# K pairs in four transfers of every fourth partition, with score matmuls that read K in whole lines

## The chip, the cores and the metric

The kernel runs on one core of one Trainium2 chip. The metric is the device time of one launch in microseconds, so lower is better. "Before" took 186.11 us (median of 3 runs, 185.71 to 186.42). For a program on one core, "slow" means over 1.5% above the fastest run of the same kernel.

## The reference

It computes two rounds of attention plus gated MLP, for 4 batches with one query token each. Cut to what matters:

```python
# B=4, D=512, Hq=32, Hkv=8, Sk=8192, Dh=128; window W = 2048 keys; all bf16
def _A_ref(x, k_cache, v_cache, wq, wo):
    q = (x @ wq).reshape(B, 1, 32, 128)
    k = k_cache[:, :, Sk - W:, :]          # repeated for 4 query heads each
    v = v_cache[:, :, Sk - W:, :]
    p = softmax(q k^T * Dh ** -0.5)
    return (p v) @ wo
x = x + _A_ref(layernorm(x), K, V, wq, wo)
x = x + glu(layernorm(x), w_gate, w_up, w_down)   # D=512, F=1792
# ... and both lines once more, with the same K, V and weights
```

K in the window is 4 x 8 x 2048 x 128 x 2 bytes = 16.8 MB, and V is the same. The kernel keeps all of K in SBUF between the two rounds, and reads nearly all of V twice.

## The kernel before

All transfers except the small input x are issued by one engine (SyncE) in a planned order. For each KV head, K comes in two *pairs* of batches, 1 MB per transfer. A pair fills 128 partitions with one 8 KB row (32 keys) each, and neighbouring partitions alternate between the two batches:

```python
def pair_d(cache, h, bp):       # DRAM side: 64 x 2 rows of 8 KB
    return cache[2 * bp:2 * bp + 2, h, SK - W:SK, :].rearrange("b (p j) d -> p b (j d)", p=64)

def load_k(h):
    where[("K", h)] = h
    for bp in range(2):
        dma("K%d_%d" % (h, bp), kpair(h, bp), pair_d(A_k, h, bp), w=tok(4 * h + 2 * bp), rate="bw_8k")
```

VectorE then transposes each tile of 128 x 1024 4-byte words in place (STREAM_TRANSPOSE on the page, 1219 ns each). The score matmuls index what it leaves as blocks in which 32 rows lie side by side along a partition. They read one batch out of the pair:

```python
for cp in range(4):
    for b in range(NB):
        gi = 2 * (b % 2) + b // 2       # four column groups of the array, one per batch
        kt = kpair(hk, b // 2).rearrange("p (j c x i t) -> p c t i j x", c=2, x=16, i=2, t=2)
        q0 = ((k2 * NB + b) * 4 + cp) * NR
        last = pe.matmul(ps[32 * gi:32 * gi + NR, bank, :], qbd[:, q0:q0 + NR],
                         kt[:, cp // 2, cp % 2, b % 2, :, :], start=(cp == 0), stop=(cp == 3))
```

Here `i` is the batch within the pair, and the innermost index `x` steps over it. Successive elements read are 8 bytes apart, so two of them fall into each 16 bytes of a partition. The texts call 16 adjacent bytes of a partition a line; here the word stands for the layout only.

Of the kernel before, what the change touches and what calls it, by code (L numbers as in the profile page):

```python
# [248 lines left out]
class _SlotPool:  # L249
# [12 lines left out]

_TM = dict(
    sem_lat=100.0, pick_tol=60.0,
    dma_issue=60.0, dma_lat0=900.0, dma_lat1=1100.0, dma_max_out=16,
    bw_8k=430.0, bw_4k=412.0, bw_3k=409.0, bw_1k=356.0,
    pe_pair=38.0, pe_small=230.0, pe_f32=450.0, pe_row=80.0, pe_sq=300.0,
    dve_fix=150.0, dve_f32=1.04, dve_small=90.0,
# [4 lines left out]
def build(nc, A_x, A_k, A_v, A_wq, A_wo, B_wg, B_wu, B_wd, out, cfg=None):  # L273
    cfg = dict(cfg or {})
# [4 lines left out]
    KEEP_V = cfg.get("KEEP_V", 2)  # L279
    NG = len(GROUPS)  # L280
    assert GROUPS == [[0, 1, 2, 3]]
    N_DMA_SEMS = cfg.get("N_DMA_SEMS", 24)

    NB, SQ, D = A_x.shape
    _, HKV, SK, DH = A_k.shape
    HQ = A_wq.shape[1] // DH
    REP = HQ // HKV
    W = min(4096, max(256, SK // 4))
# [26 lines left out]
    with es:  # L315
# [35 lines left out]
        eng_sems = dict((e, es.enter_context(nc.semaphore("s_" + e))) for e in ENGINES if e != "sync")  # L351
        dma_sems = [es.enter_context(nc.semaphore("s_dma%d" % i)) for i in range(N_DMA_SEMS)]

# [10 lines left out]
        def slot_ap(s):  # L364
            return arena[:, s * SLOT:(s + 1) * SLOT]

        def tile_ap(s):
            return arena[:, s * SLOT:(s + 2) * SLOT]

        def tok(s):  # L370
            return [("slot", s), ("slot", s + 1)]

        def c_dve(n, rate=None):
            return tm["dve_fix"] + n * (tm["dve_f32"] if rate is None else rate)

        def c_act(n):
            return tm["act_fix"] + n * tm["act_el"]

        def dma(name, dst, src, w, r=(), rate="bw_4k", nbytes=None, sem=None):
            if nbytes is None:  # L380
                nbytes = dst.partition_size() * dst.free_nbytes()
            o = P.op("sync", name, 0.0, lambda e, dst=dst, src=src: e.dma_start(dst, src),  # L382
                     r=r, w=w, dma_bytes=nbytes, dma_rate=tm[rate])
            if sem is not None:
                o.sem = sem
                o.inc = 16
            return o
# [23 lines left out]
        def need(name):  # L411
            while name not in where:
                take_load()
            return where[name]
# [7 lines left out]
        def pair_d(cache, h, bp):  # L422

            return cache[2 * bp:2 * bp + 2, h, SK - W:SK, :].rearrange("b (p j) d -> p b (j d)", p=64)

        def kpair(h, bp):
            return tile_ap(4 * h + 2 * bp)

        def load_k(h):
            where[("K", h)] = h  # L430
            for bp in range(2):
                dma("K%d_%d" % (h, bp), kpair(h, bp), pair_d(A_k, h, bp), w=tok(4 * h + 2 * bp), rate="bw_8k")

        def load(name, n_use, rate, part):
            left[name] = n_use
# [73 lines left out]
        def load_v(h, bp, k, n_use):  # L509
# [7 lines left out]
             r=[("ones_f",)], w=[("ident_b",)])  # L517
# [5 lines left out]
        for jh in range(2):  # L523
            for bp in range(2):
# [7 lines left out]
                     r=[("ones_f",), ("perm",)], w=[("perm", jh, bp)])  # L532
# [5 lines left out]
             r=perms, w=[("sel_f",)])  # L538
        P.op("gpsimd", "sel_b", 200.0, lambda g: g.tensor_copy(sel_b[:, :], sel_f[:, :]),
             r=[("sel_f",)], w=[("sel_b",)])  # L540
        P.op("vector", "sel_r", 100.0,
             lambda v: v.tensor_reduce(sel_r[:, :], sel_f[:, :].rearrange("p (g r) -> p r g", g=4), AXX, ALU.add),
             r=[("sel_f",)], w=[("sel_r",)])
# [4 lines left out]
             r=[("sel_r",)], w=[("maskr",)])  # L548
# [111 lines left out]
        def q_unit(tag, h, k2):  # L660

            for a in range(4):
                dst = qbd[32 * a:32 * a + 32, k2 * 256:(k2 + 1) * 256].rearrange(
                    "p (x y) -> p x y", y=NR)[:, :, a * REP:(a + 1) * REP]
                src = qrep[32 * a:32 * a + 32, h * 64:(h + 1) * 64].rearrange("p (x r) -> p x r", r=REP)
                rd = [("qrep", h // 4)]
                if a % 2 == 0:
                    P.op("vector", "qe%s_%d" % (tag, a), c_dve(64), lambda v, dst=dst, src=src: v.tensor_copy(dst, src),  # L668
                         r=rd, w=[("q", k2, a)])
                else:  # L670
                    P.op("scalar", "qe%s_%d" % (tag, a), c_act(64), lambda s_, dst=dst, src=src: s_.copy(dst, src),  # L671
                         r=rd, w=[("q", k2, a)])

        def k_transpose(h):
            need(("K", h))
            for t in range(4):
                v32 = slot_ap(4 * h + t).bitcast(F32)
                P.op("vector", "T%d_%d" % (h, t), c_dve(1024), lambda v, v32=v32: v.transpose(v32, v32),  # L678
                     r=[("slot", 4 * h + t)], w=[("slot", 4 * h + t)])

        ucount = [0]

        def softmax_unit(tag, hk):
            u = ucount[0]
            ucount[0] += 1
            k2 = u % 2
            bank = SB[k2]
            q_unit(tag, hk, k2)

            def e_s(pe):  # L690
                last = None
                for cp in range(4):
                    for b in range(NB):
                        gi = 2 * (b % 2) + b // 2
                        kt = kpair(hk, b // 2).rearrange("p (j c x i t) -> p c t i j x", c=2, x=16, i=2, t=2)
                        q0 = ((k2 * NB + b) * 4 + cp) * NR
                        last = pe.matmul(ps[32 * gi:32 * gi + NR, bank, :], qbd[:, q0:q0 + NR],  # L697
                                         kt[:, cp // 2, cp % 2, b % 2, :, :], start=(cp == 0), stop=(cp == 3))
                return last
            P.op("tensor", "S" + tag, 16 * tm["pe_row"], e_s,  # L700
                 r=[("slot", 4 * hk + t) for t in range(4)] + [("q", k2, a) for a in range(4)],
                 w=[("pss", k2)], banks=(bank,))
            mk = mxt[:, k2 * 32:(k2 + 1) * 32]
            P.op("vector", "mx" + tag, c_dve(512),
                 lambda v: v.tensor_reduce(nmax[:, k2:k2 + 1], ps[:, bank, :], AXX, ALU.max),  # L705
                 r=[("pss", k2)], w=[("mx", k2)], banks=(bank,))
            P.op("vector", "mk" + tag, tm["dve_small"],
                 lambda v: v.tensor_scalar(mk, maskr[:, :], nmax[:, k2:k2 + 1], None, ALU.add),
                 r=[("mx", k2), ("maskr",)], w=[("mk", k2)])
            P.op("vector", "nm" + tag, tm["dve_small"],  # L710
                 lambda v: v.tensor_reduce(nmax[:, 2 + k2:3 + k2], mk, AXX, ALU.max, negate=True, apply_transpose=True),  # L711
                 r=[("mk", k2)], w=[("nm", k2)])
            P.op("scalar", "ex" + tag, c_act(512) + 200.0,
                 lambda a: a.activation(prow[:, :].rearrange("p (m x t) -> p m x t", x=16, t=2),  # L714
                                        ps[:, bank, :].rearrange("p (m t x) -> p m x t", x=16, t=2), ACTF.Exp, bias=nmax[:, 2 + k2:3 + k2], scale=1.0,
                                        accum_out=psm[:, k2:k2 + 1]),
                 r=[("pss", k2)] + [("nm", k2)], w=[("prow",), ("psm", k2)], banks=(bank,))
            return k2
# [84 lines left out]
        def attn(L):  # L803
            hs = list(range(HKV)) if L == 0 else list(range(HKV))[::-1]

            def front(ui):
                h = hs[ui]
                if L == 0:
                    k_transpose(h)
                k2 = softmax_unit("%d.%d" % (L, ui), h)  # L810
                if L == 2:
                    for bp in range(2):
                        pool.release(4 * h + 2 * bp)
                    fill()
                return k2
# [133 lines left out]
        for h in range(2):  # L949
            loads.append((("K", h), lambda _, h=h: load_k(h)))  # L950
        for h in range(HKV):
            if h + 2 < HKV:
                loads.append((("K", h + 2), lambda _, h=h + 2: load_k(h)))
            if h % 2 == 0:
                load_wo(h // 2)
            for bp in range(2):
                load_v(h, bp, 0, 2 if (h, bp) in keep else 1)
# [25 lines left out]
        order = _schedule(P.ops, tm)  # L983
        counts = _assign_sync(P.ops, order, N_DMA_SEMS)

# [32 lines left out]
def bass_interleave_layers__sliding_block_cached__glu_gated_glu__decode_kernel(  # L1018
    nc, A_x, A_k_cache, A_v_cache, A_wq, A_wo, B_x, B_w_gate, B_w_up, B_w_down, out,
):  # L1020
    build(nc, A_x, A_k_cache, A_v_cache, A_wq, A_wo, B_w_gate, B_w_up, B_w_down, out)
# [28 lines left out]
```

## Time and profile before

| | before |
|---|---|
| time | 186.11 us |
| span of the profiled run | 184.4 us |
| SyncE's transfers (q1), busy share of 16 engines' span | 97.2% |
| bytes moved by q1 | 71.84 MB |
| TensorE busy | 101.2 us (55%) |
| a K or V row of 8 KB on its engine (packet records, median) | 309 to 311 ns |

The page cuts the span into 40 slices: the busy share of the 16 transfer engines in tenths, and what they moved. Below is the slice view with the queue's own line.

```profile
...
DMA  5999999999999999999999999999999999999980
GB/s 198 425 427 427 425 403 391 411 421 419 409 387 425 419 421 403 392 419 419 400 391 414 412 407 393 403 350 417 330 396 419 419 423 416 418 416 402 412 341 24
...
q1 hardware_dynamic: 15352, 71.84, 97.2%
...
```

The queue is full (9) from the second slice on until the last two.

Next, the costliest groups of the page that touch K: score matmuls (L697), the transposes (L678) and the row maximum behind the scores (L705). After the bar come busy us and the mean ns of one, then the idle time before them and who ended it.

```profile
...
L697 PE MATMUL ps<-arena,qbd 128*16 128x512 bf16 x256 | 32.5, 626 | 16.9 <-DVE qbd L668 8.4
...
L678 DVE STREAM_TRANSPOSE arena<-arena 128x1024 f32<-128x1024 f32 x32 | 37.9, 1219 | 3.3 <-DMA arena<-in_A_k_cache_dram 3.0
L705 DVE TENSOR_REDUCE nmax<-ps 128x1 f32<-128x512 f32 x16 | 11.0, 687 | 26.0 <-PE ps L697 26.0
...
```

A busy sum of 32.5 us for score matmuls looks like a target. The chain of waits at the end of the kernel (start, duration, what) shows why it is not one:

```profile
...
164.46 0.89 PE ps L770 x31
165.35 15.77 DMA arena<-in_B_w_down_dram
181.13 0.04 issue
181.17 0.60 PE ps L905 x8
...
```

At 165.35 us a group of matmuls of the second attention ends, and one of the last transfers of weights can be issued. It lands 15.77 us later, behind what is already queued. TensorE meanwhile finishes the attention and does most of the last MLP. With less TensorE time before that point this transfer could be issued earlier, but the transfer engines are full until 178 us (share 1.02 from 165 to 178 us, 0.99 to 1.04 in windows of 2 to 3 us there) and have the same bytes to deliver. So nearly nothing should be won. The page's issue table shows the K transfers (count, KB each, median us from issue to landing):

```profile
...
arena<-in_A_k_cache_dram SPq DMA_DIRECT2D x16, 1024.0 KB, 16.0
...
```

### The profile page before, as it was taken

The page shows a single profiled execution, that of the slowest core. Times are in us where ns is not written, and L with a number is a line of the kernel's source. Part 1 is how long each engine was busy: PE and PEld are TensorE (multiplying, and loading weights), DVE is VectorE, ACT ScalarE, POOL GpSimd, SP SyncE. Part 2 cuts the span into 40 slices and gives each one's busy share as a digit, 9 for nine tenths or more (in the row PEclk, how much of TensorE's full clock was granted, in tenths as well). Part 3 has the DMA queues.
Part 4 walks back from the last instruction along what each step waited for, and adds up shares of the span by engine and source line. Part 5 has one row for each costly group of instructions (what it writes and reads, how often), then busy time and mean ns, then how long its engine had stood idle before and what let it go on. Part 6 is the DMA issues. An engine that isn't in the chain of part 4 may idle for free.

```text
span 184.4 us, 4421 instructions
## 1 busy us (share of the span) xinstructions
PE 101.2 (55%) x1944; PEld 54.7 (30%) x1944; DVE 89.5 (49%) x221; ACT 35.7 (19%) x100; POOL 14.8 (8%) x77
## 2 busy tenths in 40 slices
PE   0532423652807327173373545445979997994474
PEld 0101000332303323023232441210334653584422
DVE  5209998477592565925621531138463442340330
ACT  2003022240212103011020001001365442220010
POOL 4000000110000101010010000000022111120000
PEclk9999995585766756755555555555897897885569
DMA  5999999999999999999999999999999999999980
GB/s 198 425 427 427 425 403 391 411 421 419 409 387 425 419 421 403 392 419 419 400 391 414 412 407 393 403 350 417 330 396 419 419 423 416 418 416 402 412 341 24
DMA packets 15379, 72.12 MB, mean 391 GB/s; under 512 B 1144, under 2 KB 5248, under 8 KB 8704
## 3 DMA queue, kind: packets, MB, share of 16 engines
q1 hardware_dynamic: 15352, 71.84, 97.2%
q8 instruction: 15, 0.25, 0.5%
q14 instruction: 4, 0.03, 0.0%
q10 hardware_dynamic: 8, 0.00, 0.0%
HBM read 71.83 MB, written 0.00 MB: 390 GB/s over the span
## 4 chain that ended last, share of the span: by engine, by line
DMA 52%; PE 25%; SPq 16%; DVE 4%; issue 2%; ACT 0%
DMA arena<-in_A_v_cache_dram 33%; SPq L382 16%; PE ps L697 11%; DMA arena<-in_B_w_down_dram 9%; PE ps L770 8%; DMA arena<-in_A_wq_dram 5%; DMA arena<-in_B_w_up_dram 5%; PE ps L726 2%; PE ps L794 1%; DVE ps L492 1%; PE ps L626 1%; DVE nmax L705 1%; PE ps L749 1%; PE ps L905 1%; PE ps L852 1%
## 5 line engine op out<-in xcount | busy, mean ns | idle before, releaser
L770 PE MATMUL ps<-ebuf,arena 128*128 128x8 bf16 x1024 | 31.0, 167 | 29.7 <-DMA arena<-in_A_v_cache_dram 22.1
L697 PE MATMUL ps<-arena,qbd 128*16 128x512 bf16 x256 | 32.5, 626 | 16.9 <-DVE qbd L668 8.4
L770 PEld LDWEIGHTS ps<-ebuf,arena 128*128 128x128 bf16 x1024 | 28.8, 101 | 36.3 <-DMA arena<-in_A_v_cache_dram 32.5
L678 DVE STREAM_TRANSPOSE arena<-arena 128x1024 f32<-128x1024 f32 x32 | 37.9, 1219 | 3.3 <-DMA arena<-in_A_k_cache_dram 3.0
L705 DVE TENSOR_REDUCE nmax<-ps 128x1 f32<-128x512 f32 x16 | 11.0, 687 | 26.0 <-PE ps L697 26.0
L714 ACT ACTIVATE prow<-ps,nmax 128x512 bf16<-128x512 f32 x16 | 11.0, 687 | 39.6 <-DVE nmax L711 24.9
L671 ACT COPY qbd<-qrep 32x64 bf16<-32x64 bf16 x32 | 7.7, 241 | 40.9 <-PE ps L697 40.3
L697 PEld LDWEIGHTS ps<-arena,qbd 128*16 128x16 bf16 x256 | 6.1, 97 | 31.3 <-issue 22.0
L739 POOL CAST s<-psm 128x1 bf16<-128x1 f32 x16 | 3.0, 188 | 144.4 <-ACT prow L714 144.4
L778 DVE TENSOR_TENSOR onb<-ps,rinv 128x16 bf16<-128x16 f32 x16 | 2.9, 184 | 21.1 <-PE ps L770 21.1
L626 PE MATMUL ps<-arena,xn 128*4 128x512 bf16 x64 | 7.8, 582 | 7.6 <-DMA arena<-in_A_wq_dram 6.2
L794 PE MATMUL ps<-onb,arena 128*128 128x4 bf16 x256 | 9.1, 166 | 3.1 <-DVE onb L778 3.1
L731 ACT CAST prow<-ps 128x512 bf16<-128x512 f32 x16 | 9.4, 587 | 7.1 <-PE ps L726 7.0
L735 DVE STREAM_TRANSPOSE ebuf<-prow 128x256 f32<-128x256 f32 x16 | 7.0, 437 | 6.7 <-ACT prow L731 6.4
L852 PE MATMUL ps<-arena,xn 128*4 128x448 bf16 x64 | 6.5, 560 | 4.9 <-DVE xn L607 3.1
L794 PEld LDWEIGHTS ps<-onb,arena 128*128 128x128 bf16 x256 | 7.9, 101 | 4.1 <-DVE onb L778 2.8
L726 PE MATMUL ps<-prow,perm 64*128 64x256 bf16 x64 | 7.4, 315 | 2.4 <-ACT prow L714 2.3
L596 ACT ACTIVATE lnv<-lnv 128x4 f32<-128x4 f32 x4 | 0.8, 205 | 34.0 <-DVE lnv L593 34.0
L634 DVE STREAM_TRANSPOSE ebuf<-ps 128x512 f32<-128x512 f32 x4 | 2.9, 715 | 7.7 <-PE ps L626 7.6
L859 DVE STREAM_TRANSPOSE ebuf<-ps 128x448 f32<-128x448 f32 x4 | 2.6, 650 | 7.8 <-PE ps L852 7.8
L668 DVE COPY qbd<-qrep 32x64 bf16<-32x64 bf16 x32 | 5.3, 166 | 0.7 <-ACT qrep L657 0.2
L749 PE MATMUL ps<-sel_b,s 128*128 128x16 bf16 x48 | 3.8, 175 | 3.2 <-POOL s L743 2.4
(61 smaller groups left out, 68.1 us busy)
## 6 DMA issues: line engine op xcount, KB each, us to landing
arena<-in_A_v_cache_dram SPq DMA_DIRECT2D x30, 1024.0 KB, 16.8
arena<-in_A_k_cache_dram SPq DMA_DIRECT2D x16, 1024.0 KB, 16.0
arena<-in_A_wq_dram SPq DMA_DIRECT2D x8, 1024.0 KB, 9.4
arena<-in_A_wo_dram SPq DMA_DIRECT2D x4, 1024.0 KB, 24.3
arena<-in_B_w_gate_dram SPq DMA_DIRECT2D x4, 896.0 KB, 19.7
arena<-in_B_w_up_dram SPq DMA_DIRECT2D x4, 896.0 KB, 15.8
arena<-in_B_w_down_dram SPq DMA_DIRECT2D x2, 1024.0 KB, 12.5
arena<-in_B_w_down_dram SPq DMA_DIRECT2D x1, 768.0 KB, 7.0
```

Source lines behind the costliest of these rows:

```text
L382: o = P.op("sync", name, 0.0, lambda e, dst=dst, src=src: e.dma_start(dst, src), r=r, w=w, dma_bytes=nbytes, dma_rate=tm[rate])
L626: last = pe.matmul(ps[32 * hh:32 * hh + NB, qb, :], xn[:, c * NB:(c + 1) * NB], tile_ap(s)[:, o + hh * 512:o + (hh + 1) * 512], start=(c = ...
L671: P.op("scalar", "qe%s_%d" % (tag, a), c_act(64), lambda s_, dst=dst, src=src: s_.copy(dst, src), r=rd, w=[("q", k2, a)])
L678: P.op("vector", "T%d_%d" % (h, t), c_dve(1024), lambda v, v32=v32: v.transpose(v32, v32), r=[("slot", 4 * h + t)], w=[("slot", 4 * h + t)])
L697: last = pe.matmul(ps[32 * gi:32 * gi + NR, bank, :], qbd[:, q0:q0 + NR], kt[:, cp // 2, cp % 2, b % 2, :, :], start=(cp == 0), stop=(cp = ...
L705: lambda v: v.tensor_reduce(nmax[:, k2:k2 + 1], ps[:, bank, :], AXX, ALU.max),
L714: lambda a: a.activation(prow[:, :].rearrange("p (m x t) -> p m x t", x=16, t=2), ps[:, bank, :].rearrange("p (m t x) -> p m x t", x=16, t ...
L726: last = pe.matmul(ps[:, PBS[i], 0:256], perm[64 * i:64 * i + 64, jh * 128:(jh + 1) * 128], prow[64 * i:64 * i + 64, jh * 256:(jh + 1) * 2 ...
L731: lambda a: a.copy(prow[:, :].rearrange("p (y i t) -> p i y t", i=2, t=2), ps[:, PBS[0]:PBS[0] + 2, 0:256].rearrange("p i (y t) -> p i y t ...
L770: last = pe.matmul(ps[:, ob, bp * 8:bp * 8 + 8], src[:, j * 128:(j + 1) * 128], ev[:, j % 2, j % 16 // 2, x0:x0 + 8], start=(j == 0), stop ...
L794: last = pe.matmul(ps[:, WB, c * NB:(c + 1) * NB], tile_ap(s)[:, o + r_ * D + c * 128:o + r_ * D + (c + 1) * 128], ov[:, r_ * NB:(r_ + 1) ...
L852: last = pe.matmul(ps[32 * g:32 * g + NB, OBS[n], 0:NF], xn[:, c * NB:(c + 1) * NB], tile_ap(s)[:, o:o + NF], start=(c == 0), stop=(c == N ...
```

## The change

The intent is to place four partitions of one batch side by side, so that after the transposition four keys of one batch (16 bytes with both halves of a word) are adjacent and score matmuls read K in whole lines. One even step over partitions doesn't give "four of batch 0, four of batch 1" with the batch as an inner dimension of the source. So each pair comes in four transfers, and transfer `x` fills partitions x, x+4, x+8, and so on. The semaphores and the planner's limit rise with the number of transfers.

```diff
-    ... dma_max_out=16,
+    ... dma_max_out=32,
-    N_DMA_SEMS = cfg.get("N_DMA_SEMS", 24)
+    N_DMA_SEMS = cfg.get("N_DMA_SEMS", 40)
@@ load_k
-                dma("K%d_%d" % (h, bp), kpair(h, bp), pair_d(A_k, h, bp), w=tok(4 * h + 2 * bp), rate="bw_8k")
+                src = A_k[2 * bp:2 * bp + 2, h, SK - W:SK, :].rearrange("b (y x j) d -> x y b (j d)", y=16, x=4)
+                for x in range(4):
+                    dma("K%d_%d%d" % (h, bp, x), kpair(h, bp)[x:128:4], src[x], w=[("k", 4 * h + 2 * bp, x)], rate="bw_8k")
@@ k_transpose
-                     r=[("slot", 4 * h + t)], w=[("slot", 4 * h + t)])
+                     r=[("k", 4 * h + t // 2 * 2, x) for x in range(4)], w=[("slot", 4 * h + t)])
@@ softmax_unit
-                        kt = kpair(hk, b // 2).rearrange("p (j c x i t) -> p c t i j x", c=2, x=16, i=2, t=2)
+                        kt = kpair(hk, b // 2).rearrange("p (j c y i x t) -> p c t i j y x", c=2, y=4, i=2, x=4, t=2)
-                                         kt[:, cp // 2, cp % 2, b % 2, :, :], start=(cp == 0), stop=(cp == 3))
+                                         kt[:, cp // 2, cp % 2, b % 2], start=(cp == 0), stop=(cp == 3))
```

More of the change, by code (lines that the diff above doesn't have):

```diff
@@ L264 @@
     sem_lat=100.0, pick_tol=60.0,
-    dma_issue=60.0, dma_lat0=900.0, dma_lat1=1100.0, dma_max_out=16,
+    dma_issue=60.0, dma_lat0=900.0, dma_lat1=1100.0, dma_max_out=32,
     bw_8k=430.0, bw_4k=412.0, bw_3k=409.0, bw_1k=356.0,
```

## The prediction

> **What bounds the kernel.** The DMA does. The page's slices give a DMA share of 9 tenths or more from the second slice to the next to last, and the queue table puts the SyncE queue at 97.2% of 16 engines' span, 71.84 MB. Windows of 4 us show 412 to 428 GB/s almost everywhere while 8 KB rows move, with two dips near 120 us (344) and 128 to 136 us (350). In the packet records an 8 KB row takes 309 ns on its engine and a semaphore write 9 ns. TensorE is busy 55%. The chain of waits names score matmuls (line 697) for 11%, mostly in the second attention (129 to 165 us), but that stretch is followed by a 15.8 us wait for the last weights, which the queue was delivering at full rate all the time: what TensorE saves there only lengthens the queue.
>
> **What the change removes.** Score matmuls now stream a moving operand with four of a line's elements used in a run, not two. A group of 16 lasts 1.9 to 2.0 us now, at granted clock 0.5 (46 us) and 1.0 (129 us) alike, about 480 ns per round of four column groups, so reading, not the clock, sets it.[...] My estimate is 1.0 to 1.7 us after, 0.2 to 0.9 us less in each of 16 groups, 3 to 14 us of TensorE time. Nearly none lies on the binding resource. Earlier slot releases may fill the dip near 120 us: at most 1 us.
>
> **What it adds.** 48 more transfers: 768 semaphore writes at 9 ns over 16 engines, 0.4 us. SyncE pays about 0.61 us per K issue, so 64 take about 39 us, not 10; a 256 KB piece carries 0.62 us of data at 424 GB/s, so the queue keeps its lead of several microseconds, made by wq and V. Vector transposes wait on four semaphores, not one: small.
>
> **The risk** is how 32 rows at a step of four partitions spread over engines.[...] If they collide, K rows take up to twice as long: K is 16.8 MB, 39.6 us at 424 GB/s, so 10 to 30 us more.[...] No transfer in this trace tells.
>
> **Prediction.** Without collisions 185 to 187 us; with them 200 to 215. I put somewhat more on the first: 187.0 us, 8 in 10 between 184.0 and 212.0. Faster by over 2%: 0.05; within 2%: 0.57; slower by over 2%: 0.38.
>
> **What would show it.** Score groups at 1.0 to 1.7 us; DMA share still 9 everywhere; semaphore-write packets up by 768; K issues about 0.6 us each. No collision: 8 KB rows still near 309 ns and 412 to 428 GB/s at 12 to 24 us. Collision: two populations of K rows (309 and up to 620 ns) and 250 to 350 GB/s there, VectorE transposes waiting longer for K.
>
> **What would make it wrong.** SyncE's issue cost rising for a strided destination until the queue runs dry in the first 25 us; a larger cost per small transfer than the 9 ns records show; or the middle of the kernel (104 to 136 us) being so sensitive to early releases that it gains several microseconds.

The sum of the forecast: 185 to 187 us without collisions, 10 to 30 us more with them, put as 200 to 215, and 187.0 us as the middle. The "up to twice as long" is the author's assumption; no transfer of before shows it. The estimate of 1.0 to 1.7 us for a score group is the author's too: no trace of before shows it, and it is not part of the sum (in after, 14 of 16 groups took 1.88 to 1.91 us and two 1.41 and 1.47).

## More of the kernel before

The next view gives two windows of before. The columns are the busy time of each engine with its number of instructions, the granted clock (the share of TensorE's full speed that the profile says it had), the busy share of the transfer engines, and GB/s. In the first window almost only K moves. The second lies around the gated MLP between the two attention rounds.

```profile
...
core 0: us, PE busy (x) PEld busy (x) DVE busy (x) ACT busy (x) POOL busy (x), PEclk, DMA share, GB/s
16.00:24.00 8.00, 2.42 (x32) 0.65 (x32) 7.94 (x10) 1.60 (x7) 0.00 (x0) 1.00 1.01 426
112.00:128.00 16.00, 6.95 (x114) 2.81 (x106) 5.91 (x17) 1.16 (x5) 0.00 (x0) 0.50 1.00 389
...
```

At 426 GB/s and a busy share of 1.01 the transfer engines have no idle time left.

## The result, and the profile after

The change takes **213.84 us** (median of 4 runs, 212.83 to 215.77), against 186.26 us for before in the same rounds. The ratio is 1.1502 (95% interval 1.143 to 1.1574). A ratio here is the mean time of one kernel's fast runs over that of the other's fast runs of the same rounds, so it is not quite the ratio of the medians quoted.

The slice view and queue line of after:

```profile
...
DMA  6999999999999999999999999969999999999990
GB/s 225 420 346 279 279 281 288 411 292 306 350 319 348 350 318 338 258 266 396 283 276 308 348 423 403 377 218 389 360 417 414 412 425 421 418 415 409 406 372 27
...
q1 hardware_dynamic: 16120, 71.84, 96.5%
...
```

The share is still 9 but for the ends and slice 27 (6, near 140 us), but the rate falls to between 258 and 350 GB/s in most slices from the fourth to the 23rd, while K is being loaded. When all K is in SBUF it recovers, and from the 30th slice on it is above 400 until the tail. The engines are as busy as before and move less. Windows of after: the K stretch, and the gated MLP.

```profile
...
core 0: us, PE busy (x) PEld busy (x) DVE busy (x) ACT busy (x) POOL busy (x), PEclk, DMA share, GB/s
16.00:24.00 8.00, 0.64 (x20) 0.41 (x24) 5.07 (x7) 1.27 (x5) 0.00 (x0) 1.00 1.02 281
136.00:152.00 16.00, 7.12 (x110) 3.78 (x108) 4.23 (x20) 1.57 (x7) 0.00 (x0) 1.00 0.83 311
...
```

The K stretch went from 426 to 281 GB/s. The groups that answer to those of before, and the K issues:

```profile
...
L680 DVE STREAM_TRANSPOSE arena<-arena 128x1024 f32<-128x1024 f32 x32 | 38.3, 1225 | 19.1 <-DMA arena<-in_A_k_cache_dram 19.1
...
L699 PE MATMUL ps<-arena,qbd 128*16 128x512 bf16 x256 | 29.3, 602 | 25.7 <-DVE qbd L670 13.0
L707 DVE TENSOR_REDUCE nmax<-ps 128x1 f32<-128x512 f32 x16 | 11.0, 687 | 25.5 <-PE ps L699 25.5
...
```

```profile
...
arena<-in_A_k_cache_dram SPq DMA_DIRECT2D x64, 256.0 KB, 16.8
...
```

VectorE's transposes now wait 19.1 us for K, against 3.0 us before. The score matmuls' busy sum fell only from 32.5 to 29.3 us. The packet records of the trace (one record per row on its engine; counts and durations of the SyncE queue, worked out over the records) show where the time is:

```
                    before: count  median  mean ns  sum/16      after: count  median  mean ns  sum/16
8 KB rows                   6656    311    318.5   132.50 us          6656    316    373.2   155.23 us
1 KB rows                   4100     48     50.3    12.90 us          4100     54     58.2    14.91 us
semaphore writes            1140      9      9.5     0.67 us          1908      9     12.0     1.43 us
8 KB rows, K alone:  before, 12 to 24 us, mean 310.5 ns      after, 16 to 30 us, mean 470.8 ns
```

In this first K stretch of after, all 479 rows lie between 461 and 488 ns. K has 2048 rows, or 128 for each of 16 engines (2048 / 16). If all of them were as slow, 128 x (470.8 - 310.5) ns = 20.5 us would be added; this is an estimate, since later K rows, mixed with V, scatter more. All 8 KB rows together, V included, grew by 22.7 us (155.23 - 132.50). The whole queue was busy for 179.3 us before and for 204.9 us after (the sum of all its records over 16), which is 25.7 us more. The rest of the span difference of 27.9 us is 2.2 us in which the queue was not full; the window 136 to 152 us accounts for it (share 0.83; before had 1.00 in the corresponding window). So nearly all the added time is transfer time, and K rows make about 20 us of it. All 16 engines stay busy in the K stretch (share 1.02), so it isn't that fewer engines do the work.

### The profile page after: what moved, and what is told of

Same layout as the page of the kernel before. It is cut to its first block, busy times and chain, and to the rows that moved or that the text cites. A ratio compares the mean times of both kernels' runs of the same rounds, so it can differ in the third digit from the quotient of the medians.

```text
span 212.3 us, 4510 instructions
## 1 busy us (share of the span) xinstructions
PE 102.0 (48%) x1944; PEld 56.3 (27%) x1944; DVE 90.2 (42%) x221; ACT 35.7 (17%) x100; POOL 14.7 (7%) x77
## 4 chain that ended last, share of the span: by engine, by line
SPq 44%; DMA 33%; PE 17%; issue 3%; DVE 2%; ACT 1%
SPq L382 44%; DMA arena<-in_A_v_cache_dram 16%; DMA arena<-in_B_w_down_dram 12%; PE ps L699 5%; PE ps L772 5%; DMA arena<-in_A_wq_dram 5%; PE ps L728 2%; PE ps L907 1%; PE ps L796 1%; PE ps L628 1%; PE ps L931 0%; PE ps L854 0%; PE ps L751 0%; ACT prow L716 0%; DVE ebuf L636 0%
## 5 line engine op out<-in xcount | busy, mean ns | idle before, releaser
L772 PE MATMUL ps<-ebuf,arena 128*128 128x8 bf16 x1024 | 31.6, 168 | 52.2 <-DMA arena<-in_A_v_cache_dram 49.2
L680 DVE STREAM_TRANSPOSE arena<-arena 128x1024 f32<-128x1024 f32 x32 | 38.3, 1225 | 19.1 <-DMA arena<-in_A_k_cache_dram 19.1
L772 PEld LDWEIGHTS ps<-ebuf,arena 128*128 128x128 bf16 x1024 | 29.4, 104 | 59.1 <-DMA arena<-in_A_v_cache_dram 55.5
L699 PE MATMUL ps<-arena,qbd 128*16 128x512 bf16 x256 | 29.3, 602 | 25.7 <-DVE qbd L670 13.0
L728 PE MATMUL ps<-prow,perm 64*128 64x256 bf16 x64 | 9.3, 389 | 1.4 <-ACT prow L716 1.4
L751 PEld LDWEIGHTS ps<-sel_b,s 128*128 128x128 bf16 x48 | 2.5, 106 | 8.2 <-issue 5.9
```

Of the source, the lines that this page charges most:

```text
L680: P.op("vector", "T%d_%d" % (h, t), c_dve(1024), lambda v, v32=v32: v.transpose(v32, v32), r=[("k", 4 * h + t // 2 * 2, x) for x in range( ...
L728: last = pe.matmul(ps[:, PBS[i], 0:256], perm[64 * i:64 * i + 64, jh * 128:(jh + 1) * 128], prow[64 * i:64 * i + 64, jh * 256:(jh + 1) * 2 ...
L772: last = pe.matmul(ps[:, ob, bp * 8:bp * 8 + 8], src[:, j * 128:(j + 1) * 128], ev[:, j % 2, j % 16 // 2, x0:x0 + 8], start=(j == 0), stop ...
```

## The experiments

Three theories could explain slow K rows:

- **Where rows land.** The record calls it the port theory, and the labels own_port4 and own_port4_again come from it. As a theory: what a row takes depends on the partitions that a transfer fills and on how the rows of its source are given to the engines, which could then get in each other's way. The factors of two and four on 309 ns are assumptions, which the runs test.
- **Small transfers.** 256 KB pieces of 32 rows, or the step of four, cost time in themselves.
- **Memory side.** Neighbouring source rows of a transfer are now 32 KB apart, and reading them so could take longer.

Twelve runs were made, of eleven kernels. Some compute a wrong result. The comparison with the reference passed for all of them, even where keys and values no longer match, so its tolerance does not see such errors here. That own_port4, step2 and quarters are right rests on their layouts, not on this comparison. Several kernels with slow rows scatter by more than 1.5% from run to run, so most of their runs count as "slow". Their runs are then given one by one, and the argument rests on row times and on GB/s inside the K stretch, which differ by far more. Profile lines below are the window 16 to 24 us of each run, with the columns as above. All mean row times are from the packet records in the first stretch of K; another window within it moves the slow means by up to 3 ns.

### own_port4: the same four transfers, source of one dimension

```diff
-  src = A_k[2 * bp:2 * bp + 2, h, SK - W:SK, :].rearrange("b (y x j) d -> x y b (j d)", y=16, x=4)
+  src = A_k[2 * bp:2 * bp + 2, h, SK - W:SK, :].rearrange("b (i x j) d -> b x i (j d)", i=32, x=2)
   for x in range(4):
-      dma(..., kpair(h, bp)[x:128:4], src[x], ...)
+      dma(..., kpair(h, bp)[x:128:4], src[x // 2, x % 2], ...)
@@ score matmuls (two keys of a batch side by side)
+  kt = ... "p (j c y i x t) -> p c t i j y x", c=2, y=8, i=2, x=2, t=2
```

> Still 64 K transfers of 256 KB to every fourth partition, but each takes its 32 rows from one batch, so that the source has one dimension of 32 rows, not 16 x 2. Port theory[...] K rows back to about 309 ns, K stretches at 415 to 430 GB/s, time 185 to 189 us. Small-transfer theory (256 KB pieces or the step of four themselves cost it): K rows stay near 470 ns, 210 to 215 us. Memory-side theory (rows of 16 engines 32 KB apart are slow to read): 16 KB apart here, so some relief, rows 309 to 470 ns.

```profile
...
16.00:24.00 8.00, 2.38 (x32) 0.61 (x32) 7.94 (x10) 1.49 (x6) 0.00 (x0) 1.00 1.02 423
...
```

K rows took 310 ns on average, and the stretch ran at 423 GB/s. The time was 184.71 us (183.94 to 185.5) against 185.91 for before, ratio 0.9944 (0.9896 to 0.9991). There are as many transfers, of the same size, to the same partitions, with as many semaphore writes and issues as in the change, and nothing of the loss is left. The small-transfer theory falls.

### quarters: four transfers to neighbouring partitions

```diff
-  .rearrange("b (y x j) d -> x y b (j d)", y=16, x=4)
+  .rearrange("b (x y j) d -> x y b (j d)", y=16, x=4)
-  kpair(h, bp)[x:128:4]
+  kpair(h, bp)[32 * x:32 * x + 32]          # score reads as before
```

> Four transfers per pair again, but each fills 32 neighbouring partitions with the same pair layout as before, so the result is right and score reads are as before. Port theory:[...] K rows about 618 ns (twice 309), 222 to 230 us. Small-transfer theory: the same as the change, rows 470 ns, 210 to 215 us. Memory-side theory:[...] rows 309 ns, 185 to 189 us.

```profile
...
16.00:24.00 8.00, 0.79 (x32) 0.49 (x32) 3.66 (x5) 1.71 (x6) 0.00 (x0) 1.00 1.02 218
...
```

Rows took 602 ns on average, at 218 GB/s. The time was 234.04 us (232.79 to 237.92, of which the last counts as slow), ratio 1.2576 (1.2512 to 1.264). A transfer fills 32 neighbouring partitions here, and the rows take nearly twice 309 ns (1.95 times). The time is over the expected range. The row time is a little under 618.

### near_source: the change with source rows 8 KB apart (wrong result)

```diff
-  .rearrange("b (y x j) d -> x y b (j d)", y=16, x=4)
+  .rearrange("b (x y j) d -> x y b (j d)", y=16, x=4)      # destination as in the change
```

> The change with the source rows of one transfer 8 KB apart and not 32 KB (the result is wrong on purpose: keys and values no longer match). Destination and number of transfers as in the change. Port theory and small-transfer theory: nothing changes, K rows 470 ns, 211 to 217 us. Memory-side theory: K rows near 309 ns, 185 to 190 us.

```profile
...
16.00:24.00 8.00, 0.55 (x20) 0.41 (x24) 5.14 (x7) 1.33 (x5) 0.00 (x0) 1.00 1.02 279
...
```

Rows took 473 ns at 279 GB/s, the same as in the change. The fast runs are 209.05 and 211.70 us, ratio 1.1325 (1.1224 to 1.1426). The other two, and the profiled one among them, count as slow at 212.39 and 213.84. The distance of the rows in memory is not the cause of slow rows. The pair near_source and quarters says more: both read the same source rows in the same cut, and fill other partitions. Rows took 473 ns in one and 602 ns in the other, so it counts where the rows land.

### big_16x8 and big_32x4: whole 1 MB transfers (wrong result)

Both read the same 1 MB of one batch into all 128 partitions with one transfer. They differ only in how the source is cut.

```diff
-  dma(..., kpair(h, bp), pair_d(A_k, h, bp), ...)
+  dma(..., kpair(h, bp), A_k[2 * bp, h, SK - 2 * W:SK, :].rearrange("(r y j) d -> y r (j d)", r=8, y=16), ...)   # big_16x8
+  dma(..., kpair(h, bp), A_k[2 * bp, h, SK - 2 * W:SK, :].rearrange("(r y j) d -> y r (j d)", r=4, y=32), ...)   # big_32x4
```

> The kernel before, with each K transfer whole (1 MB, 128 partitions, 16 transfers in all), but its source given as 16 x 8 rows that cannot be merged (8 KB apart and 128 KB apart; wrong result on purpose). Port theory:[...] K rows slow, mean 400 to 500 ns, perhaps in two populations near 309 and 618, 198 to 218 us. Small-transfer theory and memory-side theory: rows 309 ns, 185 to 189 us.

```profile
...
16.00:24.00 8.00, 0.40 (x16) 0.27 (x16) 4.00 (x5) 1.30 (x5) 0.00 (x0) 1.00 1.01 229
...
```

> The twin of big_16x8: the same 1 MB of one batch per transfer, the same 128 partitions, but the source given as 32 x 4 rows and not 16 x 8 (wrong result on purpose). Port theory[...]: K rows about 309 ns, 420 GB/s, 185 to 188 us. If it is the rows' distance in memory or a source of two dimensions that made big_16x8 slow: rows 500 ns and more, 220 us and more.

```profile
...
16.00:24.00 8.00, 2.42 (x32) 0.67 (x32) 7.94 (x10) 1.60 (x7) 0.00 (x0) 1.00 1.01 424
...
```

With 16 x 8 rows: 573 ns on average (440 to 630), 229 GB/s, and runs of 225.00 (fast), 230.54, 235.50 and 240.92 us. The row time is over the expected 400 to 500, and so is the time over its 198 to 218. With 32 x 4 rows: 311 ns, 424 GB/s, 186.04 us (185.34 to 186.95), ratio 0.9983 (0.9921 to 1.0045). Neither small pieces nor a step over partitions is needed for the loss, and a source of two dimensions is harmless. For transfers like these the number in the slowest source dimension decides: 16 is slow, and 32 or more is not. Numbers between were not tried.

### step2 and step2_16x4: two transfers of every second partition

```diff
@@ step2 (right result)
+  src = A_k[2 * bp:2 * bp + 2, h, SK - W:SK, :].rearrange("b (y x j) d -> x y b (j d)", y=32, x=2)
+  for x in range(2): dma(..., kpair(h, bp)[x:128:2], src[x], ...)
@@ step2_16x4 (wrong result): one batch, 16 x 4 rows
+  src = A_k[2 * bp:2 * bp + 2, h, SK - W:SK, :].rearrange("b (r y j) d -> b y r (j d)", r=4, y=16)
+  for x in range(2): dma(..., kpair(h, bp)[x:128:2], src[x], ...)
```

> Two transfers of 512 KB per pair to every second partition, source 32 x 2 rows (right result; two keys of one batch side by side). Port theory:[...] K rows about 309 ns, 185 to 189 us. If any step over partitions or any split were what costs: rows between 309 and 470 ns, 195 to 213 us.

```profile
...
16.00:24.00 8.00, 2.40 (x32) 0.65 (x32) 7.89 (x10) 1.51 (x6) 0.00 (x0) 1.00 1.01 423
...
```

> The twin of step2: two transfers of 512 KB to every second partition, the source of each given as 16 x 4 rows of one batch and not 32 x 2 (wrong result on purpose).[...] The runs so far fit 618 n - 150 ns[...] (470 for n = 1, 573 a row for n = 4), so 543 ns a row here, between 530 and 555, about 240 GB/s, 220 to 228 us. Two-row pieces or the step as causes: 309 ns as in step2, or 470.

```profile
...
16.00:24.00 8.00, 0.40 (x16) 0.27 (x16) 4.12 (x6) 1.56 (x6) 0.00 (x0) 1.00 1.00 231
...
```

step2 has rows of 311 ns, 423 GB/s, 185.12 us (185.11 to 185.89) and ratio 0.9984 (0.9954 to 1.0014). step2_16x4 has rows of 560 ns, 231 GB/s, and runs of 218.84 (fast), 223.52, 228.41 (the profiled one) and 232.63 us. The destination and the number of transfers are the same in both, and again 16 against 32 decides. The expected 543 ns from the fit "618 n - 150" missed by 17 ns, just outside its range. In that fit n is 1 for 16 x 2 source rows, 2 for 16 x 4 and 4 for 16 x 8, and the formula is the time of n rows. It was the author's estimate from the 470 and 573 ns of two kernels (for n = 4 it gives 580), and why it should hold was not shown.

### k01_16rows: 16 rows to 16 neighbouring partitions (wrong result, heads 0 and 1 only)

```diff
+  for x in range(8 if h < 2 else 0):
+      src = A_k[2 * bp + x // 4, h, SK - W + x % 4 * 512:SK - W + x % 4 * 512 + 512, :]
+      dma(..., kpair(h, bp)[16 * x:16 * x + 16], src.rearrange("(y j) d -> y (j d)", y=16), ...)
   # K of heads 2 to 7 as before
```

> The kernel before, but the K pairs of heads 0 and 1 alone come in 8 transfers of 16 rows to 16 neighbouring partitions each (wrong result on purpose).[...] Port theory: these rows take about four times 309, 1236 ns, 106 GB/s while K of heads 0 and 1 arrives, 10 us of data take 40; all later rows 309 ns; 210 to 225 us.[...]

```profile
...
16.00:40.00 24.00, 2.66 (x48) 0.79 (x40) 8.75 (x11) 2.19 (x8) 0.00 (x0) 0.93 1.03 147
...
```

Here the window is 16 to 40 us. Rows of these heads took about 896 ns on average (28 to 32 us) at 147 GB/s. Later rows were back near 313 ns. The times are 202.22 us (fast) and 205.33 us (slow, the profiled run). Transfers to 16 neighbouring partitions are far worse than those to 32 (602 ns in quarters). But 896 ns is 2.9 times 309, not four times, and 202 us is under the expected 210: the size that the theory gave was missed.

### reads_only and loads_only: the two halves of the change (both wrong results)

```diff
@@ reads_only: before, with the score matmuls' read order of the change
@@ loads_only: the change, with the score matmuls' read order of before
```

> The kernel before with only the score matmuls' read order of the change (wrong result on purpose). Theory: DMA bounds the kernel, so 185 to 187.5 us. Score groups: where the clock is at half a round of four takes the 427 ns[...], groups 1.88 us as in the change; where it is up, about 340 ns and 1.4 us, not 450 ns and 2.0 us as before. If score matmuls did count: 180 to 184 us.

Score matmuls in the timeline of TensorE (start, us, then the group, x16 is a whole group). First before, then reads_only, then after, in the second attention (the two lines near 27 us are of the first). L726 is another group, for comparison.

```profile
...
133.93 0.39 PE L726 MATMUL ps<-prow,perm 64*128 64x256 bf16 x4 [0.34 <-ACT prow L714]
134.49 2.00 PE L697 MATMUL ps<-arena,qbd 128*16 128x512 bf16 x16 [0.16 <-DVE qbd L668]
...
```

```profile
...
26.70 1.88 PE L697 MATMUL ps<-arena,qbd 128*16 128x512 bf16 x16 [3.86 <-DVE qbd L668]
28.52 0.61 PE L726 MATMUL ps<-prow,perm 64*128 64x256 bf16 x4
...
133.71 0.39 PE L726 MATMUL ps<-prow,perm 64*128 64x256 bf16 x4 [0.28 <-ACT prow L714]
134.26 1.15 PE L697 MATMUL ps<-arena,qbd 128*16 128x512 bf16 x16 [0.17 <-DVE qbd L668]
...
138.63 1.16 PE L697 MATMUL ps<-arena,qbd 128*16 128x512 bf16 x16
...
148.08 1.88 PE L697 MATMUL ps<-arena,qbd 128*16 128x512 bf16 x16
...
```

```profile
...
160.66 1.47 PE L699 MATMUL ps<-arena,qbd 128*16 128x512 bf16 x16
...
163.34 1.41 PE L699 MATMUL ps<-arena,qbd 128*16 128x512 bf16 x16
...
167.98 1.88 PE L699 MATMUL ps<-arena,qbd 128*16 128x512 bf16 x16
...
```

reads_only took 186.28 us (185.68 to 187.22), ratio 1.004 (0.9998 to 1.0083): no gain. Its groups do get shorter. Inside a 1.88 us group of reads_only the rounds of four matmuls (one for each column group) start mostly 427 ns apart. In three groups that start between 134 and 143 us they begin 215 to 246 ns apart, and those groups take 1.15 to 1.32 us. They are shorter than the 340 ns expected. Before has rounds of 410 to 475 ns, near 445 on average, in nearly all its groups, at 134 us as well. Was the clock the same there? The L726 group just ahead serves as a gauge. In before it takes 0.39 us where the granted clock is 1.00 (at 39 and 134 us) and 0.61 us where it is 0.50 (at 82 and 142 us). At 134 us it took 0.39 us in both runs, against 0.61 us at 28.52 us in reads_only, where rounds take 427 ns. So with four keys of a batch side by side rounds took 215 to 246 ns where L726 took 0.39 us, and 427 ns where it took 0.61 us. Before stayed near 445 ns in both cases (412 to 443 ns at 46 us, clock 0.50; 431 to 455 ns at 134 us, clock 1.00). The kernel does not care.

In after the granted clock is 0.65 from 160.7 to 167.5 us, where rounds take 246 to 359 ns, and 0.50 from there until 208 us, with rounds of 427 ns after the first of a group. Earlier the clock of the page does not agree with the durations. In after it reads 1.00 at 24 us, where a score group takes 1.89 us. The slice view of reads_only, below, shows a full clock for its first 31 slices, while the ten score groups before 133 us have rounds of 427 ns, as have those at 148 to 157 us where the view shows half.

```profile
...
PEclk9999999999999999999999999999999555555558
...
```

> The change with the score matmuls' old read order (wrong result on purpose). All theories of the loss lying in the loads: 211 to 217 us, the time of the change. If the new read order gave anything back, this is slower than the change by that much.

```profile
...
16.00:24.00 8.00, 0.41 (x16) 0.28 (x16) 4.97 (x6) 1.13 (x5) 0.00 (x0) 1.00 1.02 263
...
```

Rows took 499 ns at 263 GB/s, 28 ns more than the same transfers took in the change; this scatter is not explained. The runs are 208.02 (fast), 211.46, 212.43 and 213.37 us (the last is the profiled one). The loads alone make essentially the whole loss. Whether the new read order gave back or cost a microsecond can't be told from these runs.

### plan_only and own_port4_again

plan_only is before with the two raised constants. own_port4_again repeats own_port4 with more rounds.

> The kernel before with 40 transfer semaphores and the planner's limit of 32 transfers in flight, no other edit. Theory: nothing, 185.5 to 187 us. If these constants reorder the transfers to effect: more than 1% either way.

185.68 us (185.46 to 186.01), ratio 1.0007 (0.9976 to 1.0037): the constants do nothing.

> own_port4 again with more rounds: its ratio of 0.9944 (0.9896 to 0.9991) may be a small gain or chance. If real, 0.990 to 0.998 again; if chance, an interval that holds 1.

186.69 us (185.69 to 187.25, 6 runs), ratio 1.0012 (0.9968 to 1.0056). The small gain of the first run did not come again, so it is put down to chance. No version found here beats before.

### What follows from all of them

| kernel | source rows | destination | K row, ns | GB/s |
|---|---|---|---|---|
| before | 64 x 2 | 128 | 311 | 426 |
| own_port4 | 32 | 32, step 4 | 310 | 423 |
| step2 | 32 x 2 | 64, step 2 | 311 | 423 |
| big_32x4 | 32 x 4 | 128 | 311 | 424 |
| **after** | 16 x 2 | 32, step 4 | 471 | 281 |
| loads_only | 16 x 2 | 32, step 4 | 499 | 263 |
| near_source | 16 x 2 | 32, step 4 | 473 | 279 |
| step2_16x4 | 16 x 4 | 64, step 2 | 560 | 231 |
| big_16x8 | 16 x 8 | 128 | 573 | 229 |
| quarters | 16 x 2 | 32 neighbours | 602 | 218 |
| k01_16rows | 16 | 16 neighbours | 896 | 147 |

The shape of the source decides between 311 ns and slow. That is shown by pairs with the same destination and number of transfers (big_32x4 and big_16x8, step2 and step2_16x4). They also differ in how far apart the source rows lie, which made no difference in near_source. quarters and k01_16rows don't belong to this comparison: their transfers fill 32 and 16 neighbouring partitions, where the others fill a span of all 128. They test what the destination costs: 602 and 896 ns. That it costs something by itself rests on the pair near_source and quarters, where the same source rows took 473 and 602 ns on other partitions. That engines get in each other's way there, as the theory has it, was not shown. The trace does not record which engine wrote which partition.

Two things stay open. One is why the rows are slow, and why they are all near 470 ns in the first stretch of the change, instead of a mixture of 309 and 618. The other is the few microseconds beyond the K rows: 1 KB rows went from 50.3 to 58.2 ns, and the queue was no longer full around 140 us. Both are seen in the trace and were not tried alone.

## Why the prediction was wrong

1. *DMA bounds the kernel*: right. reads_only makes score groups shorter and gains nothing (1.004).
2. *"0.2 to 0.9 us less in each of 16 groups"*: in after, 14 of 16 groups last 1.88 to 1.91 us, some 0.1 us less than before, and only two are clearly shorter (1.47 and 1.41 us). The limit by reading was rightly seen (rounds near 445 ns also at 134 us, where the granted clock is 1.00 and L726 is at its fast 0.39 us; the 480 ns of the prediction is a group's whole length over four). But nearly everywhere else rounds take 427 ns even with whole lines, hardly less than before. From 168 us on that is at a granted clock of 0.50, with the group that answers to L726 (L728) at 0.61 us; for the groups before 160 us a lower clock is the author's reading, from L728 groups of 0.61 us there too; the page shows 1.00. In reads_only at 134 us, where L726 takes 0.39 us, the saving is 0.85 us (1.15 against 2.00 us). It had no weight for the time.
3. *What it adds*: 768 semaphore writes more: counted (1908 against 1140). They made 0.8 us more in after, where one took 12.0 ns on average and not 9.5, and 0.4 us in own_port4. K issues about 0.59 us each: as said. own_port4 pays both and loses nothing.
4. **The step that failed**: *"Without collisions 185 to 187 us; with them 200 to 215. I put somewhat more on the first: 187.0 us."* The collision was named, and then given the smaller chance. The runs show the loss that belongs to it: rows of 471 ns, 281 GB/s, 213.84 us, inside the stated 200 to 215 for that case and above the upper end of 212.0 for the whole. That rows collide was not shown, as said above; that a source with 16 in its slowest dimension makes them slow is (573 against 311 ns in big_16x8 and big_32x4, 560 against 311 ns in step2_16x4 and step2). The alternative, that nothing is lost, holds in the runs with 32 or more in the slowest source dimension (310 to 311 ns), and not in those with 16.
5. *"K rows take up to twice as long, 10 to 30 us more"*: measured 1.52 times and about 20.5 us (estimate) for K rows, and 27.6 us in all (213.84 - 186.26). *"Two populations of K rows (309 and up to 620 ns)"*: wrong for the first stretch, where there is one near 470. The 281 GB/s there and the longer waits of the transposes were as said.
6. *"What would make it wrong"* listed SyncE's issue cost, the cost per small transfer and the middle of the kernel. None of these was it.

Seen from here, the weights were a guess. What the prediction had for the collision rested on nothing measured. For the other side it had the full speed of 64 x 2 rows in before (309 ns), which is another shape. "No transfer in this trace tells", it says itself. One run with a 16-row source would have settled what was weighed.

## What to carry to other kernels

When a transfer is cut into pieces or given a step over partitions, look at the number in the slowest dimension of its DRAM side: here 32 or more kept 8 KB rows at 310 ns, and 16 made them 470 to 575 ns, in transfers of 256 KB as in those of 1 MB. And look at the partitions that it fills: 32 neighbours took 600 ns a row and 16 neighbours 900. A full busy share of the transfer engines with fewer GB/s was the sign of it, and the durations of single rows in one profile showed it. And before making matmuls faster in a kernel whose transfer queue is full from end to end, ask what they would free: here the answer was nothing.
